# Second attention: q and k projections in three lots of eight, with paired 64-row remainders

## The chip, the cores and the metric

The kernel runs on one core of a Trainium2 chip. The metric is the device time of one execution in microseconds (us). A TensorE (PE) matmul takes a stationary operand of up to 128 x 128, loaded by a weight load (PEld), and a moving operand of up to 128 x 512; results go to PSUM, eight banks of 512 float32 values a partition. VectorE (DVE) and ScalarE (ACT) read PSUM; GpSimd (POOL) and SyncE (SP) work on SBUF and issue transfers (DMAs).

## The reference, cut to what matters

```
x = A_x
x = x + A(layernorm(x), A_wqkv, A_wo)                    # first attention
x = x + B(layernorm(x), B_w_in, B_w_sp, B_b_sp, B_w_out) # feed-forward
x = x + A(layernorm(x), A_wqkv, A_wo)                    # second attention
x = x + B(layernorm(x), B_w_in, B_w_sp, B_b_sp, B_w_out)

def A(x, wqkv, wo):      # x: 2048 x 576, 32 heads of 18, window of 8 positions, dilation 2
    q, k, v = split(x @ wqkv)
    logits = q . k[pos - 2*(0..7)] * scale, masked where the position is negative
    return (softmax(logits) @ v[pos - 2*(0..7)]) @ wo

def B(x, w_in, w_sp, b_sp, w_out):
    z1, z2 = split(gelu(x @ w_in)); g = w_sp @ layernorm(z2) + b_sp
    return (z1 * g) @ w_out
```

## The kernel before

Four layers, A B A B, run one after the other. The normalised input stands transposed in `xnT`: 128 partitions, five chunks of the 576 features, 2048 positions. Four chunks are full; the fifth has 64 features. Its lower 64 partitions hold either a copy of the upper 64 (where the writer of the rows makes one, `dup`) or zeros; `wqk4`, the fifth chunk of the q and k weights, has zeros in its lower 64 rows, so that a full-height matmul of chunk five gives the product of 64 rows.

In an attention layer the engines' order is written by hand. Its pieces:

- `PG(d, qk, cc, ...)`, one unit of the q and k projection: for 128 of the 576 output columns (d = 0 to 4; at d = 4, one unit gives the last 64 of q and of k), q or k, and 512 positions (cc = 0 to 3), five matmuls into one PSUM bank (L436), a copy of the bank into a staging buffer `stg` (`evac`, ACT L404 or DVE L402), and, when all units of a d over 1024 positions are there, about eight DMAs that move each head's 18 rows into `QK` (L78), dealt to the SP and POOL queues. There are four staging buffers, used in turn; a copy into one waits until the moves out of it have landed.
- `fill_window_rows`, DVE copies of a mask pattern into `QK` (L198, L202); the moves into `QK` come after them.
- `VW(t, hh)`, a v product: five matmuls of 288 columns (L410) and a copy into `v_ext`, in this stage on ACT (L404).
- `L_mm(s)`, logits of half a tile: 16 matmuls of 32 rows (L473) into the three-bank buffer `X0` and one "Y" bank; `EXP(s)`, two exponentials on ACT (L482); `PV(s)`, the weighted sum (L496) and the division on DVE.

PSUM in an attention layer: three banks for `X0` (0 to 2), two "Y" (3, 4) and three "PT" (5, 6, 7). `PT_tile` takes a bank for a unit or a v product by the tags in `self.ring`: Y, Y, PT, PT, PT at first, PT alone from the line in front of `L_mm(0)` on. Which buffer of a tag is taken is settled when the program is built.

The second attention (li = 2) starts with 18 units (d = 0 to 4, cc = 0 and 1), then eight v products (tiles 0 to 3), then `L_mm(0)` and `EXP(0)`, then six more units (d = 0 to 2, cc = 2, the list `pre`), then a loop over the steps: at each, `L_mm(s + 1)`, `EXP(s + 1)`, `PV(s)` and what a table puts there (the remaining units, v products, output projection, layer norm).

Ahead of it, the output stage of the first feed-forward (L1104) writes the rows of `xnT` tile by tile: sums, statistics, normalised rows on ACT (`ln_xn`, L253), transposition by DMA. In it the second attention's weights are loaded through ACT's DMA queue (`late_loads`), and `zero_right` (L297) zeroes the lower rows of three weights on DVE.

The feed-forward's first product (`z1`, L1031, and `p1_group`, L907) has the form that the change takes up: chunks one to four of half of the units, then chunk five of all units as half-height matmuls at rows 0 and 64 in turn, which address the two halves of the array, then chunks one to four of the other half.

Of the kernel before, what the change touches and what calls it, by code (L numbers as in the profile page):

```python
# [12 lines left out]
f32 = mybir.dt.float32  # L13
# [5 lines left out]
P = 128  # L19
# [44 lines left out]
class K:  # L64
# [229 lines left out]
        wv = wp.tile([P, 5, D], bf16, name="wv_sb")  # L294
        self.right = dict(pf_cm=pf_cm, w_cm=w_cm, pf=pf, win2a=win2a, wqk=wqk, wqk4=wqk4, wv=wv, wo=wo)

    def zero_right(self):  # L297
        nc, R = self.nc, self.right
        nc.vector.memset(R["wqk4"][64:128, :], 0.0)
        nc.vector.memset(R["wv"][64:128, 4, :], 0.0)  # L300
        nc.vector.memset(R["wo"][64:128, 4, :], 0.0)

    def load_wqk(self, eng):

        R = self.right
        for c0, n, w0 in ((D, 512, D + 64), (0, D, 0), (D + 512, 64, D)):
            self.dma(R["wqk"][:, :, w0:w0 + n], self.A_wqkv[0:512, c0:c0 + n].rearrange("(c p) n -> p c n", p=P), eng=eng)
            self.dma(R["wqk4"][:64, w0:w0 + n], self.A_wqkv[512:576, c0:c0 + n], eng=eng)

    def load_wv(self, eng, nh=1):  # L310
        R, n = self.right, D // nh
# [27 lines left out]
    def layer_A(self, li):  # L339
# [33 lines left out]
        R = self.right  # L373
# [26 lines left out]
        def evac(out, in_, dve):  # L400
            if dve:
                nc.vector.tensor_copy(out=out, in_=in_)  # L402
            else:
                nc.scalar.copy(out=out, in_=in_)  # L404
# [9 lines left out]
        stg_tiles, stg_left = {}, {}  # L414
        dma_rr, stg_rr = [0], [0]

        def PG(d, qk, cc, dve, queues=(nc.sync, nc.gpsimd)):

            cb, gi = divmod(cc, CBW // 512)
            alone = bool(lent) and d == 4 and cb == 1  # L420
            key = (d, cc if alone else cb, alone)
            if key not in stg_tiles:
                if alone:
                    stg_tiles[key] = lent[1]
                elif cb == 0 and d >= 3 and lent:
                    stg_tiles[key] = lent[d - 3]
                else:
                    stg_tiles[key] = stgs[stg_rr[0] % NSTG]
                    stg_rr[0] += 1
                stg_left[key] = 1 if alone else (2 if d < 4 else 1) * (CBW // 512)  # L430
            stg = stg_tiles[key]
            pp = self.PT_tile([P, 512], f32, "pp")
            w0 = d * P + (640 if qk else 0)
            for c in range(5):
                w = wqk[:, c, w0:w0 + P] if c < 4 else wqk4[:, w0:w0 + P]
                nc.tensor.matmul(pp[:, :], lhsT=w, rhs=self.xnT[:, c, cc * 512:(cc + 1) * 512],  # L436
                                 start=(c == 0), stop=(c == 4))
            evac(stg[:, qk, gi * 512:(gi + 1) * 512], pp[:, :], dve)
            stg_left[key] -= 1
            if stg_left[key] == 0:  # L440
                stg_tiles.pop(key)
                cs = slice(cc * 512, (cc + 1) * 512) if alone else slice(cb * CBW, (cb + 1) * CBW)
                ss = slice(gi * 512, (gi + 1) * 512) if alone else slice(0, CBW)
                moves = []
                for h in range(d * P // DH, H):
                    a, b = max(h * DH, d * P), min((h + 1) * DH, (d + 1) * P)
                    if a >= b:
                        break
                    g, rg = divmod(h, 4)
# [153 lines left out]
        if li == 0:  # L603
# [44 lines left out]
            xns = {}  # L648
# [72 lines left out]
            T_(12, 13, 14, 15)  # L721
            nvw0, nvw = 4, 9
        else:
            for k_, (d, cc) in enumerate([(d, cc) for d in range(5) for cc in range(2)]):
                for qk in ((1, 0) if d < 4 else (0,)):
                    PG(d, qk, cc, k_ == 0, (nc.gpsimd, nc.sync) if d == 0 else q2)
                if k_ == 0:
                    self.fill_window_rows(QK, 0)
                    setup_bufs(nc.vector)
                    nc.vector.memset(v_ext[:, :, :, DH:DH + 1], 1.0)  # L730
                    exp_table()
                if k_ == 1:
                    self.run_deferred()
                if k_ == 6:
                    self.fill_window_rows(QK, 1)
            nvw0, nvw = 0, 4
        for t in range(nvw0, nvw - (1 if li == 0 else 0)):
            for hh in range(2):
# [74 lines left out]
            at(s_b + 2 * k_, win2b_piece, k_)  # L813
        at(NST - 2, O_T, NT - 2)
        at(NST, O_T, NT - 1)
        for k_, (d, qk, cc) in enumerate(pre):
            if k_ == (2 if li == 0 else 0):
                self.ring = ["PT"]
                L_mm(0)
                EXP(0)  # L820
            PG(d, qk, cc, li > 0 or k_ < 4, q2)
            if li == 0 and k_ == 3:
                self.fill_window_rows(QK, 1)
# [24 lines left out]
    def layer_B(self, li):  # L848
# [231 lines left out]
        late_loads = []  # L1080
        if next_is_A:
            self.open_right()
            late_loads = [lambda: self.load_wqk(nc.scalar),
                          lambda: self.load_wv(nc.scalar), lambda: self.load_wo(nc.scalar)] + self.load_win2a(nc.scalar)
        xns = {}

# [21 lines left out]
        def p3_finish(i, acc):  # L1108
            xo = p3.tile([P, D], f32, name="xo3", bufs=3)
            self.dma(xo[:], self.rows_of(x_prev, i) if next_is_A else x_prev[i * P:(i + 1) * P, :], eng=nc.sync)  # L1110
            x_new = p3.tile([P, D], bf16 if last else f32, name="x_new3", bufs=3)
            for hh in range(2):
                hs = slice(hh * 288, (hh + 1) * 288)
                nc.vector.tensor_tensor(out=x_new[:, hs], in0=acc[hh], in1=xo[:, hs], op=ALU.add)  # L1114
                if last:
                    self.dma(self.out[i * P:(i + 1) * P, hs], x_new[:, hs], eng=(nc.sync, nc.scalar)[hh])
            if not last:
                self.dma(self.xres[li][i * P:(i + 1) * P, :], x_new[:])
                mv, rstd, nmr = self.ln_stats(p3, x_new, P)
                xns[i] = self.ln_xn(x_new, P, mv, rstd, nmr, eng="act", dup=False)  # L1120
            if i >= 2 and (i - 2) in xns:
                p3_ln_T(i - 2)()

# [11 lines left out]
        for i in range(i0, NS):  # L1135
            pos_ = [self.PT_tile([P, 512], f32, "po") for hh in range(2)]
            acc = [pos_[0][:, 0:288], pos_[1][:, 0:288]]
            p3_mm(i, acc, range(NJ))
            p3_finish(i, acc)
            if next_is_A and i == 2:  # L1140
                self.zero_right()
            if i >= 3 and late_loads:
                late_loads.pop(0)()
        if (NS - 2) in xns:
# [72 lines left out]
```

## Time and profile before

| what | value |
|---|---|
| median of 3 runs | 1165.69 us (1164.6 to 1165.92) |
| profiled execution, first to last instruction | 1170.2 us |
| PE busy | 1150.5 us, 98% of the span, 8163 instructions |
| DVE, ACT, POOL busy | 550.0, 338.8, 278.8 us |
| PE, matmuls of the q and k units (L436), both attentions | x341, 82.2 us, mean 382 ns |
| mean granted PE clock | 0.997 of full |

The profiled execution's own time is known through its span alone; it is 4.5 us above the runs' median. A matmul's recorded length holds its way through the array, so consecutive ones overlap: the pitch from start to start is what counts. A line of the timeline gives start, length, engine, line of the kernel, operation, output and inputs, form, count, and in brackets the idle time before and what ended it. Times are us from the span's start. Some matmul records are missing.

### The profile page before, as it was taken

To read this page: it belongs to the slowest core of one execution; us is meant where nothing else is said; L and a number is where in the kernel's file an instruction comes from. 1 tells how busy PE (TensorE), PEld (TensorE's weight loads), DVE (VectorE), ACT (ScalarE), POOL (GpSimd) and SP (SyncE) were. 2 spreads that over 40 slices of the span, in tenths; PEclk is the share of its full clock that TensorE was granted. 3 is DMA by queue.
4 is the path that set the end of the run, shared out by engine and by line. 5 is a ranking of instruction groups with operands and counts; after the bars stand their busy time and mean duration, and the time that the engine had idled before them with its cause. 6 is when DMAs were issued, how large, how long until landed. Compare 5 with 4: busy or idle time off the path is not lost.

```text
span 1170.2 us, 19968 instructions
## 1 busy us (share of the span) xinstructions
PE 1150.5 (98%) x8163; PEld 612.5 (52%) x8258; DVE 550.0 (47%) x1167; ACT 338.8 (29%) x493; POOL 278.8 (24%) x389
## 2 busy tenths in 40 slices
PE   9999999999999999999999999999999999999998
PEld 5457544444444444457755774444444444444677
DVE  8668598322333332244555886963322223322321
ACT  5589455111100111101247884541011110111000
POOL 4659865000000000001153786640000000000000
PEclk9999999999999999999999999999999999999999
DMA  9599697000000000049646997930000000001332
GB/s 217 119 160 294 193 212 142 23 12 12 12 1 12 12 12 1 6 138 296 169 107 105 204 256 182 242 91 1 12 12 12 12 12 1 12 1 46 111 105 74
DMA packets 183240, 106.45 MB, mean 91 GB/s; under 512 B 135225, under 2 KB 164441, under 8 KB 183149
## 3 DMA queue, kind: packets, MB, share of 16 engines
q1 hardware_dynamic: 170285, 84.85, 31.6%
q0 software_dynamic: 6512, 14.57, 4.8%
q10 hardware_dynamic: 6352, 5.75, 1.6%
q8 instruction: 64, 1.05, 0.4%
q14 instruction: 27, 0.22, 0.1%
HBM read 42.40 MB, written 21.77 MB: 55 GB/s over the span
## 4 chain that ended last, share of the span: by engine, by line
PE 85%; POOL 7%; DMA 3%; DVE 2%; issue 2%; ACT 0%; SPq 0%; POOLq 0%; DVEq 0%; ACTq 0%
PE pg L1055 42%; PE po L1104 12%; PE pz L1031 6%; PE pz1s L1031 6%; PE pzs L907 5%; PE pp L436 4%; PE pz L907 4%; POOL ln_xn L259 4%; PE pv L410 2%; PE O_ps L496 1%; PE pw L557 1%; PE L_ps L473 1%; POOL ln_rstd L582 1%; DMA QK<-stg 1%; DMA o_slot<-o_t 1%
## 5 line engine op out<-in xcount | busy, mean ns | idle before, releaser
L1055 PE MATMUL pg<-Wq,Z 128*128 128x512 bf16 x2260 | 497.9, 379 | 2.5
L1055 PEld LDWEIGHTS <-Z 128*128 128x128 bf16 x2304 | 225.5, 98 | 271.8
L1059 DVE TENSOR_TENSOR g_tmp<-pg,ln_xn 128x512 f32<-128x512 f32 x144 | 99.6, 692 | 421.5 <-PE pg L1055 419.5
L1050 ACT ACTIVATE z1T<-pz 128x1024 bf16<-128x1024 f32 x36 | 34.9, 1021 | 500.8 <-PE pz L1031 500.8
L78 POOL DMA_DIRECT2D wout<-in_B_w_out_dram x4 | 4.3, 1070 | 598.8 <-PE pg L1055 598.8
L1104 PE MATMUL po<-wout,Z 128*128 128x288 bf16 x1152 | 141.4, 286 | 0.0
L482 ACT ACTIVATE P_sb<-L_ps 128x1440 bf16<-128x1440 f32 (+3 forms) x136 | 125.1, 972 | 21.1 <-PE L_ps L473 19.7
L1104 PEld LDWEIGHTS <-Z 128*128 128x128 bf16 x1152 | 112.7, 98 | 28.8
L907 PEld LDWEIGHTS <-xnT 128*128 128x128 bf16 (+1 forms) x800 | 68.7, 98 | 80.0 <-issue 15.5
L1060 DVE TENSOR_TENSOR Z<-g_tmp,z1T 128x512 bf16<-128x512 f32 x144 | 99.7, 692 | 12.2
L956 DVE BATCH_NORM_STATS2 z_st<-zp 128x6 f32<-128x512 bf16 (+1 forms) x160 | 91.0, 617 | 5.1 <-ACT zp L954 4.8
L1031 PEld LDWEIGHTS <-w 128*128 128x128 bf16 (+1 forms) x640 | 53.7, 97 | 74.0 <-issue 13.6
L436 PE MATMUL pp<-xnT,wqk_sb 128*128 128x512 bf16 x341 | 82.2, 382 | 2.5 <-DVE o_t L504 1.3
L259 POOL TENSOR_SCALAR ln_xn<-x_new,ln_mv,ln_rstd 128x576 bf16<-128x576 f32 x32 | 73.3, 2291 | 2.6
L1114 DVE TENSOR_TENSOR x_new<-po,xo 128x288 f32<-128x288 f32 (+1 forms) x64 | 28.8, 455 | 87.4 <-PE po L1104 83.9
L1031 PE MATMUL pz<-xnT,w 128*128 128x512 bf16 (+1 forms) x316 | 66.3, 380 | 0.2
L1031 PE MATMUL pz1s<-xnT,w 128*128 128x512 bf16 (+1 forms) x310 | 64.9, 379 | 0.9 <-issue 0.8
L78 POOL DMA_DIRECT2D QK<-stg x81 | 49.5, 614 | 46.0 <-DVE oT L524 14.8
L907 PE MATMUL pzs<-win2a,xnT 128*128 128x512 bf16 (+1 forms) x235 | 59.9, 364 | 0.4 <-issue 0.3
L907 PE MATMUL pz<-win2a,xnT 128*128 128x512 bf16 (+1 forms) x233 | 58.3, 357 | 0.6 <-issue 0.2
L980 POOL TENSOR_SCALAR Z<-zp,z_mv,z_rstd 128x256 bf16<-128x256 bf16 x32 | 55.7, 1740 | 3.4
L436 PEld LDWEIGHTS <-wqk_sb 128*128 128x128 bf16 x360 | 33.5, 98 | 38.3 <-DVE o_t L504 1.5
(113 smaller groups left out, 936.6 us busy)
## 6 DMA issues: line engine op xcount, KB each, us to landing
xres<-x_new SPq DMA_DIRECT2D x48, 288.0 KB
xo<-xres SPq DMA_DIRECT2D x32, 288.0 KB
wout<-in_B_w_out_dram POOLq DMA_DIRECT2D x4, 1296.0 KB, 8.2
xn_rows<-ln_xn SPq DMA_DIRECT2D x32, 160.0 KB
w<-in_B_w_in_dram SPq DMA_DIRECT2D x16, 256.0 KB
QK<-stg POOLq DMA_DIRECT2D x55, 72.0 KB, 5.2
xo<-xres SPq DMA_DIRECT2D x6, 576.0 KB
QK<-stg SPq DMA_DIRECT2D x39, 72.0 KB
```

The lines of the kernel that those rows point to most:

```text
L78: return eng.dma_start(out=out, in_=in_)
L259: e.tensor_scalar(out=xn[:nrows, 0:D], in0=x_t[:nrows, :], scalar1=mv[:nrows, 0:1], scalar2=rstd[:nrows, 0:1], op0=ALU.subtract, op1=ALU.mult)
L436: nc.tensor.matmul(pp[:, :], lhsT=w, rhs=self.xnT[:, c, cc * 512:(cc + 1) * 512], start=(c == 0), stop=(c == 4))
L482: nc.scalar.activation(out=P_bufs[2 * jp + s % 2][:nk, :, :, 0:nq], in_=Lv[:nk, :, :, 0:nq], func=ACT.Exp, scale=scale)
L907: nc.tensor.matmul(out[:, o0:o0 + n], lhsT=self.xnT[r0:r1, c, r * P:(r + 1) * P], rhs=win2(c)[r0:r1, w0:w0 + n], start=start, stop=stop, t ...
L956: nc.vector.bn_stats(out=st[:, x // 512, :], in_=zp[:, x:x + min(512, w0 + n - x)])
L980: eng.tensor_scalar(out=Z[:, b0:b1, i, :], in0=zv[:, b0:b1, :], scalar1=mv[:, 0:1], scalar2=rstd[:, 0:1], op0=ALU.subtract, op1=ALU.mult)
L1031: nc.tensor.matmul(outs[a_], lhsT=w1[r0:r1, c, sub * P:(sub + 1) * P], rhs=self.xnT[r0:r1, c, q * 512:(q + 1) * 512], start=start, stop=st ...
L1055: nc.tensor.matmul(pg[:, :], lhsT=Z[:, jj, i, sub * P:(sub + 1) * P], rhs=Wq[q][:, i, :], start=(i == 0), stop=(i == NS - 1))
L1059: nc.vector.tensor_tensor(out=tmp[:], in0=pg[:, :], in1=bsp[:, qs], op=ALU.add)
L1060: nc.vector.tensor_tensor(out=uT(jj)[:, sub, qs], in0=tmp[:], in1=z1Ts[jj, sub][:, qs], op=ALU.mult)
L1104: nc.tensor.matmul(acc[hh], lhsT=u_rows(j, i), rhs=wouts[j // NJH][:, j % NJH, hh * 288:(hh + 1) * 288], start=(j == 0), stop=(j == NJ - 1))
```

## The change

In the second attention alone, the first 24 units (the 18 and the six of `pre`) are put into three lots of eight, `PG_run`. A lot takes all eight banks (`PG_banks`: the three of `X0`, and five of the ring). In it, the first four units run chunks one to four; then all eight run chunk five as half-height matmuls, units 0, 2, 4, 6 on rows 0 to 63 and units 1, 3, 5, 7 on rows 64 to 127; the first four are copied out; the last four run chunks one to four and are copied out. Lots one and two are copied by ACT, lot three by DVE.

For this the lower 64 rows of `xnT`'s fifth chunk and of `wqk4` must hold copies: `ln_xn` in the output stage before makes its copy of 64 columns (one more ACT instruction for each of 16 tiles), the three pieces of `wqk4` are loaded twice, and the DVE memset of `wqk4` goes. Behind the third lot a POOL memset zeroes `wqk4`'s lower rows, since the loop's units go on with full-height matmuls.

Around it: the window rows of the first half are filled ahead of the first unit instead of behind the second; buffer set-up, the exponential's table and the deferred transposition stand behind lot one, the window rows of the second half behind lot two. `self.ring = ["PT"]`, `L_mm(0)` and `EXP(0)` now follow lot three, and the eight v products follow them.

```diff
-    def zero_right(self):
+    def zero_right(self, wqk=True):
         nc, R = self.nc, self.right
-        nc.vector.memset(R["wqk4"][64:128, :], 0.0)
+        if wqk:
+            nc.vector.memset(R["wqk4"][64:128, :], 0.0)
...
-            self.dma(R["wqk4"][:64, w0:w0 + n], self.A_wqkv[512:576, c0:c0 + n], eng=eng)
+            for r in ((0, 64) if twice else (0,)):
+                self.dma(R["wqk4"][r:r + 64, w0:w0 + n], self.A_wqkv[512:576, c0:c0 + n], eng=eng)
...
+        def PG_mm(pp, d, qk, cc, c, start, stop, half=None):
+            w0 = d * P + (640 if qk else 0)
+            r0, r1 = (0, P) if half is None else (64 * half, 64 * half + 64)
+            w = wqk[:, c, w0:w0 + P] if c < 4 else wqk4[r0:r1, w0:w0 + P]
+            nc.tensor.matmul(pp, lhsT=w, rhs=self.xnT[r0:r1, c, cc * 512:(cc + 1) * 512],
+                             start=start, stop=stop, tile_position=(r0, 0))
+
+        def PG_run(units, banks, between=None):
+            n = len(units) // 2
+            for u in range(n):
+                for c in range(4):
+                    PG_mm(banks[u], *units[u][:3], c, c == 0, False)
+            for u in range(2 * n):
+                PG_mm(banks[u], *units[u][:3], 4, u >= n, u < n, half=u % 2)
+            for u in range(n):
+                PG(*units[u], pp=banks[u])
+            for u in range(n, 2 * n):
+                for c in range(4):
+                    PG_mm(banks[u], *units[u][:3], c, False, c == 3)
+                PG(*units[u], pp=banks[u])
+
+        def PG_banks():
+            return ([X0[:, k_, :] for k_ in range(3)] +
+                    [self.PT_tile([P, 512], f32, "pp")[:, :] for k_ in range(5)])
...
-            pp = self.PT_tile([P, 512], f32, "pp")
-            w0 = d * P + (640 if qk else 0)
-            for c in range(5):
-                w = wqk[:, c, w0:w0 + P] if c < 4 else wqk4[:, w0:w0 + P]
-                nc.tensor.matmul(pp[:, :], lhsT=w, rhs=self.xnT[:, c, cc * 512:(cc + 1) * 512],
-                                 start=(c == 0), stop=(c == 4))
-            evac(stg[:, qk, gi * 512:(gi + 1) * 512], pp[:, :], dve)
+            if pp is None:
+                pp = self.PT_tile([P, 512], f32, "pp")[:, :]
+                for c in range(5):
+                    PG_mm(pp, d, qk, cc, c, c == 0, c == 4)
+            evac(stg[:, qk, gi * 512:(gi + 1) * 512], pp, dve)
...
-            for k_, (d, cc) in enumerate([(d, cc) for d in range(5) for cc in range(2)]):
-                for qk in ((1, 0) if d < 4 else (0,)):
-                    PG(d, qk, cc, k_ == 0, (nc.gpsimd, nc.sync) if d == 0 else q2)
+            prol = [(d, qk, cc) for d in range(4) for cc in range(2) for qk in (1, 0)] + [(4, 0, 0), (4, 0, 1)]
+            prol += [(d, qk, 2) for d in range(3) for qk in (1, 0)]
+            self.fill_window_rows(QK, 0)
+            for k_ in range(0, 24, 8):
+                PG_run([(*u, k_ == 16, (nc.gpsimd, nc.sync) if u[0] == 0 and u[2] < 2 else q2)
+                        for j, u in enumerate(prol[k_:k_ + 8])], PG_banks())
                 if k_ == 0:
-                    self.fill_window_rows(QK, 0)
                     setup_bufs(nc.vector)
                     nc.vector.memset(v_ext[:, :, :, DH:DH + 1], 1.0)
                     exp_table()
-                if k_ == 1:
                     self.run_deferred()
-                if k_ == 6:
+                if k_ == 8:
                     self.fill_window_rows(QK, 1)
+            nc.gpsimd.memset(wqk4[64:128, :], 0.0)
+            self.ring = ["PT"]
+            L_mm(0)
+            EXP(0)
             nvw0, nvw = 0, 4
...
-        for k_, (d, qk, cc) in enumerate(pre):
-            if k_ == (2 if li == 0 else 0):
+        for k_, (d, qk, cc) in enumerate(pre if li == 0 else ()):
+            if k_ == 2:
                 self.ring = ["PT"]
                 L_mm(0)
                 EXP(0)
...
-            late_loads = [lambda: self.load_wqk(nc.scalar),
+            late_loads = [lambda: self.load_wqk(nc.scalar, twice=True),
...
-                xns[i] = self.ln_xn(x_new, P, mv, rstd, nmr, eng="act", dup=False)
+                xns[i] = self.ln_xn(x_new, P, mv, rstd, nmr, eng="act")
...
-                self.zero_right()
+                self.zero_right(False)
```

More of the change, by code (lines that the diff above doesn't have):

```diff
@@ L295, in open_right, with load_wqk @@
         self.right = dict(pf_cm=pf_cm, w_cm=w_cm, pf=pf, win2a=win2a, wqk=wqk, wqk4=wqk4, wv=wv, wo=wo)
-    def zero_right(self):
+    def zero_right(self, wqk=True):
         nc, R = self.nc, self.right
-        nc.vector.memset(R["wqk4"][64:128, :], 0.0)
+        if wqk:
+            nc.vector.memset(R["wqk4"][64:128, :], 0.0)
         nc.vector.memset(R["wv"][64:128, 4, :], 0.0)
         nc.vector.memset(R["wo"][64:128, 4, :], 0.0)
-    def load_wqk(self, eng):
+    def load_wqk(self, eng, twice=False):
         R = self.right
@@ L415, in layer_A, with PG @@
         dma_rr, stg_rr = [0], [0]
-        def PG(d, qk, cc, dve, queues=(nc.sync, nc.gpsimd)):
+        def PG_mm(pp, d, qk, cc, c, start, stop, half=None):
[20 more added lines that the diff above has]
+                    [self.PT_tile([P, 512], f32, "pp")[:, :] for k_ in range(5)])
+        def PG(d, qk, cc, dve, queues=(nc.sync, nc.gpsimd), pp=None):
             cb, gi = divmod(cc, CBW // 512)
```

## The prediction

> **What bounds the kernel now.** I read the chain of waits first: 85% of the span hangs on TensorE (PE).
>
> ```profile
> PE 85%; POOL 7%; DMA 3%; DVE 2%; issue 2%; ACT 0%; SPq 0%; POOLq 0%; DVEq 0%; ACTq 0%
> ```
>
> So what the change does is settled at its own place, the start of the second attention. There I read the timeline (start, length, engine, line, operation, count, idle time before).
>
> ```profile
> 592.98 19.59 PE L436 MATMUL pp<-xnT,wqk_sb 128*128 128x512 bf16 x88
> ...
> 612.40 5.06 PE L410 MATMUL pv<-wv_sb,xnT 128*128 128x288 bf16 x40
> 613.21 0.40 ACT L404 CAST v_ext<-pv 128x288 bf16<-128x288 f32 x1
> 613.83 0.40 ACT L404 CAST v_ext<-pv 128x288 bf16<-128x288 f32 x1 [0.21 <-PE pv L410]
> ...
> 617.40 0.40 PE L473 MATMUL L_ps<-QK 32*128 32x128 bf16 x16
> ...
> 617.73 6.65 PE L436 MATMUL pp<-xnT,wqk_sb 128*128 128x512 bf16 x29
> 617.84 1.94 ACT L482 ACTIVATE P_sb<-L_ps 128x1536 bf16<-128x1536 f32 x2
> ...
> 624.31 0.40 PE L473 MATMUL L_ps<-QK 32*128 32x128 bf16 x16
> ```
>
> The reader is to see five blocks back to back on PE: 18 q and k units (90 matmuls, a few of them missing from the records) from 592.98 to 612.40; eight v products, 40 matmuls, to 617.30; the first logits at 617.40; six more units from 617.73; the second logits at 624.31. One 512-column matmul costs (612.40 - 592.98)/90 = 0.216 us, a v product (617.30 - 612.40)/8 = 0.61 us. PE does not wait for ScalarE (ACT) here: the v copies follow the products at the same 0.61 us and hold nothing up. The stretch I forecast is 592.98 to 624.31, 31.33 us.
>
> A delay at 624.31 stays. From there the logits are tied to the exponentials, because one three-bank buffer holds them:
>
> ```profile
> 624.81 11.48 ACT L482 ACTIVATE P_sb<-L_ps 128x1536 bf16<-128x1536 f32 x12 [5.03 <-PE L_ps L473]
> 626.31 0.39 PE L473 MATMUL L_ps<-QK 32*128 32x120 bf16 x16
> 628.23 0.39 PE L473 MATMUL L_ps<-QK 32*128 32x120 bf16 x16
> ...
> 660.00:670.00 10.00, 10.00 (x205) 7.33 (x202) 8.71 (x31) 9.60 (x13) 7.59 (x10) 1.00 0.99 224
> ```
>
> Twelve activations, six steps, take 11.48 us without a hole, 1.91 us a step, the pitch of the logits; later PE itself is full (10.00 of 10 us from 660 to 670, the second column of that row). Neither has room to catch up, so whatever moves 624.31 moves the end.
>
> **The lots.** 24 units of five matmuls become 24 of four, plus 24 half-height matmuls in 12 pairs. The kernel already does this in the feed-forward's z1 stage, four full units, eight halves, four full units, the same 40 instructions as one lot:
>
> ```profile
> L1031 PEld LDWEIGHTS <-w x40: 93/98/99, 882.4 to 890.2; 128*128 128x128 bf16 x32, 64*128 64x128 bf16 x8
> ...
> 882.63:886.08 3.45, 3.40 (x15) 1.47 (x15) 1.00 0.01 2
> 886.18:887.05 0.87, 0.87 (x9) 0.30 (x8) 1.00 0.00 0
> 887.15:890.62 3.47, 3.47 (x18) 1.48 (x16) 1.00 0.00 0
> ```
>
> Eight halves take 0.87 us, as long as four full matmuls: the pairs do run side by side. A tenth is lost at each change of height (886.08 to 886.18, 887.05 to 887.15). A lot takes 890.62 - 882.63 = 7.99 us against 40 x 0.216 = 8.63; three lots 23.96 against 25.90. **Gain: 1.94 us**, 0.17% of the run and no more. As for bounds: with pairs that did not overlap it would be a loss of the switches, 3 x 0.2; nothing in the rows allows a gain over 12 x 0.216 = 2.6.
>
> Can the lots wait? Lot 2 needs the banks of lot 1. ACT copies eight units in a lot of 7.99 us at 0.59 each, 4.7 us, and the first four are copied while PE runs the last sixteen matmuls. Lot 3 is copied by VectorE (DVE), 8 x 0.69 = 5.5 us, into staging buffers whose moves into QK must have landed.
>
> ```profile
> 601.45 13.66 POOL L78 DMA_DIRECT2D QK<-stg  x19 [5.75 <-ACT stg L404]
> ...
> 612.65 0.59 ACT L404 CAST stg<-pp 128x512 bf16<-128x512 f32 x1 [0.55 <-PE pp L436]
> ...
> 619.08 0.69 DVE L402 CAST stg<-pp 128x512 bf16<-128x512 f32 x1 [11.06 <-DMA QK<-stg]
> ```
>
> Their issues fill the GpSimd (POOL) queue, 0.72 us each; in the new order they start one to two us earlier, since the window rows are filled ahead of the first unit. The last two copies may still wait for the moves of d = 3, as the 619.08 row shows such a wait; they guard the banks of the seventh and eighth v product only, which come late (below). Cost 0, bounds 0 to 1.5 us.
>
> **The v products, which stand outside the diff.** Before, they stood between the units, over five banks. Now they stand behind the first logits, and the ring of banks is cut to the three "PT" banks before them. In the changed program as built, the eight go to banks 5, 5, 5, 5, 5, 5, 7, 6 (before: 7, 6, 3, 4, 5, 7, 6, 3), and the second to sixth each wait for ACT:
>
> ```
> Matmult pv<-wv_sb,xnT 128x288 [waits DVE]         first
> Matmult pv<-wv_sb,xnT 128x288 [waits Activation]  second to sixth
> Matmult pv<-wv_sb,xnT 128x288 [waits DVE]         seventh, eighth
> ```
>
> So product and copy, which overlapped, alternate; and ahead of the first copy on ACT now stand the two exponentials of the first logits. Worked out on the clock of this trace: lots end at 592.98 + 23.96 = 616.94, logits at 617.04 (the 0.10 from 617.30 to 617.40), exponentials 0.44 later (617.84 - 617.40) for 1.94 us, to 619.42. The first v product (617.37) is done by then; its copy ends at 619.82. The second product starts 0.05 after it (624.81 + 1.45 = 626.26 to 626.31, where the logits waited for an exponential in the same manner; the 1.45 is the row below). From there one turn is 0.82 us from the first matmul to the copy (612.40 + 0.61 = 613.01 to 613.83), 0.40 copy and 0.05 back: 1.27 against 0.61. That a v product waits for a v copy is nothing new to this kernel: the first attention has one such wait, the 39.00 row.
>
> ```profile
> 617.84 1.45 ACT L482 ACTIVATE P_sb<-L_ps 128x1536 bf16<-128x1536 f32 x1
> ...
> 39.00 2.48 PE L410 MATMUL pv<-wv_sb,xnT 128*128 128x288 bf16 x14 [2.47 <-DVE v_ext L402]
> ```
>
> Products two to six start at 619.87, 621.14, 622.41, 623.68, 624.95; the last two follow at 0.61 and end at 626.78; the second logits start at 626.88 instead of 624.31: **+2.57 us, the gain of 1.94 already taken off** (the stall alone is 4.5). The exponential behind them is queued after the last copy, which ends (626.17 + 0.82 + 0.40 = 627.39) just as the logits are ready, so it adds nothing.
>
> **The clock.** PE then is idle from about 618.1 to 619.9, and for 0.5 of each turn of 1.27 until 625.6. The windows with the granted clock (column after the engines) show what that may bring:
>
> ```profile
> 36.71:40.12 3.41, 1.12 (x10) 0.89 (x10) 2.54 (x7) 0.31 (x1) 3.41 (x7) 1.00 0.67 167
> 40.12:43.53 3.41, 3.19 (x12) 1.62 (x11) 0.46 (x1) 0.49 (x2) 3.41 (x6) 0.50 0.77 176
> ...
> 145.94:149.35 3.41, 2.20 (x15) 0.81 (x13) 3.38 (x7) 1.84 (x4) 2.15 (x3) 1.00 0.70 139
> 149.35:152.77 3.42, 3.42 (x9) 1.21 (x9) 3.39 (x8) 1.73 (x3) 2.31 (x4) 0.50 0.52 115
> 722.80:726.21 3.41, 2.66 (x14) 1.00 (x12) 3.38 (x7) 2.28 (x4) 2.05 (x4) 1.00 0.65 136
> ...
> 147.94 1.37 PE L907 MATMUL pzs<-win2b,xnT 64*128 64x512 bf16 x5 [0.97 <-ACT zp L954]
> ```
>
> Where PE was busy 1.12 or 2.20 of 3.41 us, the next 3.41 us ran at half clock; with 2.66 busy they did not. In the new stretch a window of 3.41 us holds, by the times above, between 1.2 us (from 618 on) and some 2.3 us of work, whichever way the windows fall. So I take one window at half clock. In it a turn costs 0.61 more (its five matmuls take twice the 0.61), 1.88 us; 3.41/1.88 = 1.8 turns, **+1.1 us**. Bounds: 0, and two such windows, the second of them in the loop, up to 3.41/2 = 1.7 more.
>
> The Trainium skill, "TensorE: Matmul & The Clock Gate" (the table of what to do about the clock gate), asks only for no idle gap over about 3 us between bursts. By that rule the clock would hold here and the term would be 0; the trace speaks against it, as the 0.97 us hole at 147.94 was enough, in a window busy 64%.
>
> **Small edits.** They hang beside other work:
>
> ```profile
> L253 ACT ACTIVATE ln_xn<-x_new,ln_nmr,ln_rstd 128x576 bf16<-128x576 f32 x16 | 13.9, 867 | 87.1 <-POOL ln_nmr L243 44.7 <-DVE x_new L1114 38.9 <-DMA xres<-x_new 3.5
> ...
> L160 POOL MEMSET win_pat<- 128x528 bf16 x1 | 0.5, 538 | 0.0
> ...
> 524.14 2.94 ACTq L78 DMA_DIRECT2D wqk_sb<-in_A_wqkv_dram  x5
> ```
>
> Sixteen copies of 64 columns on ACT (under the 0.40 of a 288-column one) fit into its 87.1 us of idle there. Three more weight DMAs add 3 x 0.59 = 1.8 us to ACT's queue 60 us ahead of their use; without that cover the first layer-norm row would be late by 1.8. The POOL memset of 64 x 1152 costs 0.54 to 1.2 us by the 528-column row; it queues behind the last moves of d = 4, about 618, and the loop's first unit needs it at 628. The VectorE memset that goes away was not on the path. All 0; if one of them stood on the path, up to 1.
>
> **Sum.** -1.94 + 4.51 + 1.1 = +3.7 us. On the profiled span, 1170.2, that is 1173.9; the runs' median, 1165.69, lies 4.5 us below that span, and I lay the same difference on it: 1169.4.
>
> **The rivals.** *The clock holds* (20%): everything else as above, +2.57, 1168.3. For it: only two windows in this trace were cut, and products at 0.61 in 1.27 are close to the 2.66 that was spared. Against: the first window has the hole of 1.8 us in it. *The gain stands alone* (6%): the copies turn out not to hold PE, as in the before trace, and the lots bring 1165.69 - 1.94 = 1163.7, not slower. It decides if the v products do not share a bank; for it speaks only that no row of this stage shows such a wait, against it the order as built and the 39.00 row. *More than one window, or the copies of lot 3 late* (16%): a second window at half clock, or a staging wait that delays the first v product beyond 618.6; +5.4, 1171.1. Pairs that do not overlap are excluded by the 886.18 row.
>
> **How the numbers follow.** Forecast 58%, the rivals as given. A difference under 0.2%, 2.3 us, can't be told from no change. Slower by more: nearly all of the forecast and of the late case, 0.6 of the held clock, 85%. Within: 0.4 of the held clock and most of the lone gain, 12%. Faster: 3%, since the gain alone, 1.94, is short of the bound. The range takes in the held clock with its scatter and half of the late case: 1167.4 to 1171.6.
>
> **What would show it.** Right: pp blocks of 7.99 us a lot; the first logits 0.4 us earlier against the first unit; 1.27 us from product to product in the first six v products, "ACT v_ext" named as what PE waited for; one window of clock 0.5 behind them; the second logits 2.6 to 3.7 us later. Wrong: v products at 0.61 us, logits early by 1.9, or idle PE inside a lot, waiting for a copy or for landed moves.

## The result, and the profile after

| | median of the runs | ratio to before, 95% interval |
|---|---|---|
| before, 10 runs beside the changed kernel | 1167.32 us (1164.6 to 1170.15) | |
| changed kernel, 10 runs | 1176.17 us (1168.46 to 1184.5) | 1.008 [1.0052, 1.0109] |

The change makes the kernel 8.9 us slower, 0.8%. The forecast was 1169.4 us, 3.7 us slower, range 1167.4 to 1171.6: the direction is right, the size is not, and the time lies outside the range. The three runs of before that the forecast was laid on had a median 1.6 us under that of the ten; the rest of the miss is in the change.

The runs of the changed kernel scatter over 16 us, and with them their mean granted clock. The two at 0.999 and 1.000 took 1168.46 and 1171.71 us; the other eight, at 0.991 to 0.996, 1173.99 to 1184.5. The clock is not all of the scatter: those two differ by 3.3 us, and before's ten runs lie 5.6 us apart. The profiled run is one in the middle (span 1176.6 us, clock 0.994).

The timeline of PE over the stretch of the forecast, from the first matmul of the units to the second logits (start, length, engine, line, operation, form, count, idle time before it; units of a lot that stand in the banks of `X0` go by the name `L_ps`):

```profile
590.78 2.75 PE L423 MATMUL L_ps<-xnT,wqk_sb 128*128 128x512 bf16 x12
...
599.71 2.75 PE L423 MATMUL L_ps<-xnT,wqk_sb 128*128 128x512 bf16 x12 [0.78 <-ACT stg L406]
...
607.69 2.75 PE L423 MATMUL L_ps<-xnT,wqk_sb 128*128 128x512 bf16 x12
...
615.77 0.40 PE L498 MATMUL L_ps<-QK 32*128 32x128 bf16 x16
618.54 0.77 PE L412 MATMUL pv<-wv_sb,xnT 128*128 128x288 bf16 x5 [2.38 <-DVE stg L404]
619.80 1.00 PE L412 MATMUL pv<-wv_sb,xnT 128*128 128x288 bf16 x5 [0.49 <-ACT v_ext L406]
621.29 1.36 PE L412 MATMUL pv<-wv_sb,xnT 128*128 128x288 bf16 x5 [0.49 <-ACT v_ext L406]
...
626.83 3.76 PE L412 MATMUL pv<-wv_sb,xnT 128*128 128x288 bf16 x15 [0.49 <-ACT v_ext L406]
630.52 0.40 PE L498 MATMUL L_ps<-QK 32*128 32x128 bf16 x16
```

Before, the stretch was 31.33 us (592.98 to 624.31); now it is 630.52 - 590.78 = 39.74, 8.41 more. The profiled spans differ by less, 1176.6 - 1170.2 = 6.4 us, since outside the stretch it is the profile of before that is 2.0 us longer; it has two windows at half clock there (at 40.12 and 149.35), the changed kernel's one (at 39.95). So the loss lies in the stretch. It can be laid beside the forecast of 31.33 + 3.67 = 35.0 part by part:

| part | forecast | measured | difference |
|---|---|---|---|
| lot 1, to the first matmul of lot 2 | 7.99 | 599.71 - 590.78 = 8.93 | +0.94 |
| lots 2 and 3, to the first logits | 16.07 | 615.77 - 599.71 = 16.06 | 0 |
| logits to the second v product | 2.83 | 619.80 - 615.77 = 4.03 | +1.20 |
| second v product to the second logits | 7.01 + 1.1 | 630.52 - 619.80 = 10.72 | +2.61 |

Where the first two differences come from stands on the other engines, in the timelines of DVE, POOL and ACT:

```profile
592.35 4.62 DVE L198 COPY QK<-win_pat 128x4096 bf16<-128x4096 bf16 x4
...
592.58 2.16 POOL L239 TENSOR_TENSOR ln_rstd<-ln_rstd,neg_half 128x1 f32<-128x1 f32 x1 [3.50 <-DVE ln_rstd L238]
594.84 2.18 POOL L243 TENSOR_SCALAR ln_nmr<-ln_mv,ln_rstd 128x1 f32<-128x1 f32 x1
...
597.05 0.87 ACT L253 ACTIVATE ln_xn<-x_new,ln_nmr,ln_rstd 128x576 bf16<-128x576 f32 x1 [6.80 <-DVE QK L202]
...
598.10 1.55 ACT L406 CAST stg<-L_ps 128x512 bf16<-128x512 f32 x3
...
600.43 11.04 POOL L78 DMA_DIRECT2D QK<-stg  x15 [3.41 <-ACT stg L406]
...
617.20 1.29 DVE L404 CAST stg<-pp 128x512 bf16<-128x512 f32 x2 [2.78 <-DMA QK<-stg]
```

The window rows, now filled ahead of the first unit, are copied by DVE just while POOL does two steps on a single column for the last row tile of the layer norm. Each takes 2.2 us. So that tile's `ln_xn` starts at 597.05. Before, it started 0.95 us after POOL's first step (595.73 - 594.78), which would be 593.53 here: 3.5 us late. The copies of lot 1 stand behind it in ACT's order and start at 598.10, lot 2 waits for its first bank, and the moves out of staging start 600.43 - 590.78 = 9.65 us behind the first matmul (before: 601.45 - 592.98 = 8.47). The bracket of 597.05 names DVE because its last fill ended at about the same time as POOL's step; what the activation reads is `ln_nmr`.

Late moves make DVE's copies of lot 3 late. The two at 617.20, of the fifth and sixth unit, waited for moves to land, and the first v product takes the bank of the sixth unit. That is the hole of 2.38 us at 618.54.

The last difference is the clock. Windows of 3.41 us: PE, PEld, DVE, ACT and POOL busy, then the granted clock, DMA share, GB/s:

```profile
616.80:620.22 3.42, 1.19 (x9) 0.82 (x9) 1.29 (x2) 1.80 (x3) 2.49 (x5) 1.00 0.42 90
620.22:623.63 3.41, 2.43 (x11) 1.20 (x10) 1.29 (x2) 0.80 (x2) 0.43 (x1) 0.50 0.01 2
623.63:627.05 3.42, 2.44 (x11) 1.21 (x10) 0.00 (x0) 0.80 (x2) 0.00 (x0) 0.50 0.00 0
627.05:630.46 3.41, 3.41 (x15) 1.89 (x13) 0.00 (x0) 0.80 (x2) 0.00 (x0) 0.50 0.00 0
```

Three windows at half clock, 10.24 us, cover nearly all of the time from the second v product to the last. A turn, one product and its copy one after the other on bank 5, takes 1.85 us in them (623.14 to 624.99, say) instead of the first one's 1.26 (618.54 to 619.80).

### The profile page after: what moved, and what is told of

The parts are those of the page before. It is cut to its first block, busy times and chain, and to the rows that moved or that the text cites. A ratio compares the mean times of both kernels' runs of the same rounds, so it can differ in the third digit from the quotient of the medians.

```text
span 1176.6 us, 20068 instructions
## 1 busy us (share of the span) xinstructions
PE 1156.6 (98%) x8258; PEld 611.7 (52%) x8258; DVE 549.2 (47%) x1166; ACT 341.8 (29%) x509; POOL 282.0 (24%) x390
## 3 DMA queue, kind: packets, MB, share of 16 engines
q8 instruction: 64, 1.05, 0.4%
## 4 chain that ended last, share of the span: by engine, by line
PE 84%; POOL 7%; DMA 4%; DVE 3%; issue 1%; ACT 1%; SPq 0%; DVEq 0%; POOLq 0%; ACTq 0%
PE pg L1085 42%; PE po L1134 12%; PE pz L1061 6%; PE pz1s L1061 6%; PE pzs L937 5%; PE pz L937 5%; POOL ln_xn L259 3%; PE pv L412 2%; DMA QK<-stg 2%; POOL QK L78 2%; PE pp L423 1%; PE O_ps L521 1%; PE pw L582 1%; DVE QK L198 1%; PE L_ps L498 1%
## 5 line engine op out<-in xcount | busy, mean ns | idle before, releaser
L423 PE MATMUL pp<-xnT,wqk_sb 128*128 128x512 bf16 (+1 forms) x315 | 73.1, 381 | 1.3 <-DVE o_t L529 1.3
L412 PE MATMUL pv<-wv_sb,xnT 128*128 128x288 bf16 x340 | 55.0, 304 | 7.6 <-DVE v_ext L404 2.6
```

The costliest lines, as they stand in the source:

```text
L412: nc.tensor.matmul(pv[:nk, 0:288], lhsT=self.xnT[:, c, k0_(t):k0_(t) + nk], rhs=wv_sb[:, c, hh * 288:(hh + 1) * 288], start=(c == 0), stop ...
L423: nc.tensor.matmul(pp, lhsT=w, rhs=self.xnT[r0:r1, c, cc * 512:(cc + 1) * 512], start=start, stop=stop, tile_position=(r0, 0))
```

## The experiments

The stretch, first matmul of the units to second logits, is read in each profile in the same way; the loop behind it goes on at 1.91 us a step. A stretch is that of one profile, a median that of four (e4_busy), five (e6_turns) or eight to twelve runs; the profiled runs of e1_banks and e2_nmr were the fastest of their kernels, 3.2 and 2.7 us under the median. Against the kernel before:

| | edit | stretch | against 31.33 | median against before's beside it | ratio |
|---|---|---|---|---|---|
| after | | 39.74 | +8.41 | +8.85 | 1.008 [1.0052, 1.0109] |
| e1_banks | v products on four banks | 35.00 | +3.67 | +4.09 | 1.0047 [1.0028, 1.0065] |
| e2_nmr | last `ln_nmr` on DVE, ahead of the fill | 33.81 | +2.48 | +2.76 | 1.0033 [1.0018, 1.0048] |
| e3_both | both | 30.70 | -0.63 | -1.91 | 0.9989 [0.9975, 1.0003] |
| e4_busy | after, gaps of PE filled | 38.09 | +6.76 | +5.88 | 1.0061 [1.0046, 1.0076] |
| e5_full | e3_both without pairs | 31.34 | +0.01 | -1.04 | 1.0 [0.9981, 1.0019] |
| e6_turns | after, only the turns filled | 37.07 | +5.74 | +5.20 | 1.0042 [1.0023, 1.0061] |
| e7_queue | e3_both, some moves issued by ACT | 33.67 | +2.34 | +3.97 | 1.003 [1.0016, 1.0045] |
| e8_order | e3_both, two v copies on DVE | 29.74 | -1.59 | -2.08 | 0.9978 [0.9963, 0.9992] |
| e9_fill | before, only the fill moved ahead | 32.99 | +1.66 | +1.28 | 1.0012 [0.9992, 1.0031] |

### The v products on four banks

```diff
+                bk = PG_banks()
...
-                        for j, u in enumerate(prol[k_:k_ + 8])], PG_banks())
+                        for j, u in enumerate(prol[k_:k_ + 8])], bk)
...
-                VW(t, hh, li == 0 and hh == 0)
+                VW(t, hh, li == 0 and hh == 0, bk[4 + (2 * t + hh) % 4] if li > 0 else None)
```

> The eight v products go round the last four banks of lot 3 (4, 5, 7, 6) instead of bank 5. Theory (the stretch lost its time to four things: last row of the layer norm late 0.9, copies of lot 3 late behind the moves out of staging 1.2, turns of product and copy, half clock in those turns): lot 2 still idles 0.8 us, the first and the third v product still wait for VectorE's copies of lot 3 (some 2 and 4.5 us behind the logits), but none waits for a v copy; from the third on 0.61 us each; first pp matmul to second logits 34 us instead of 39.74, clock 0.5 in one window at most, median about 1170. Rival (the half clock comes from the hole behind the logits and not from the turns): v products at 1.2 us each, two or three windows of 0.5, stretch 36 to 38, median 1173.

The timeline of PE in e1_banks:

```profile
613.10 1.39 PE L413 MATMUL pp<-wv_sb,xnT 128*128 128x288 bf16 x10 [1.88 <-DVE stg L404]
615.78 5.11 PE L413 MATMUL pp<-wv_sb,xnT 128*128 128x288 bf16 x30 [1.30 <-DVE stg L404]
620.82 0.40 PE L499 MATMUL L_ps<-QK 32*128 32x128 bf16 x16
```

The window at half clock in it:

```profile
615.03:618.44 3.41, 2.66 (x12) 1.64 (x12) 1.29 (x2) 0.47 (x2) 0.58 (x1) 0.50 0.04 11
```

No v product waits for a v copy any more; the first and the third wait for DVE, as the theory has it. Six products at 0.61 would take 3.7 us and took 5.1: one window at half clock, in which PE still had 2.66 us of work. The stretch is 1 us longer than expected, the median 1170.99 instead of some 1170. Sharing bank 5 costs 39.74 - 35.00 = 4.74 us here, with the part of the clock that hangs on it; the holes alone cost one window.

### The last row of the layer norm

```diff
-        nc.gpsimd.tensor_scalar(out=nmr[:nrows, :], in0=mv[:nrows, 0:1], scalar1=rstd[:nrows, 0:1], scalar2=-1.0,
+        (nmr_eng or nc.gpsimd).tensor_scalar(out=nmr[:nrows, :], in0=mv[:nrows, 0:1], scalar1=rstd[:nrows, 0:1], scalar2=-1.0,
...
-                mv, rstd, nmr = self.ln_stats(p3, x_new, P)
+                mv, rstd, nmr = self.ln_stats(p3, x_new, P, nmr_eng=nc.vector if i == NS - 1 else None)
```

On DVE the `ln_nmr` step (586.85 to 587.06) waits for POOL's first step, and the fill stands behind it: it now starts at 586.98, when POOL's first step (586.27, 0.55 us) is done.

> Only the last row's ln_nmr moves from GpSimd to VectorE, ahead of the window rows' fill in VectorE's order, so that the fill can't run beside GpSimd's two small steps. Theory: ln_rstd takes 0.55 us again instead of 2.16, the last ln_xn starts 3.5 us earlier, lot 2 follows lot 1 without the 0.78 us of idle (8.0 a lot), the moves out of staging start 2 us earlier and the first v product starts within 0.5 us of the logits; the turns of 1.27 to 1.85 stay. Stretch 39.74 - 0.9 - 1.2 = 37.6, less if a half-clock window goes with it (36); median 1173 to 1174.5. Rival (the copies of lot 3 are late for the number of moves, not for their start): lot 2 without idle, but first v product still 2.4 us behind the logits, stretch 38.8, median 1175.

Timelines of POOL and of PE in e2_nmr:

```profile
586.27 0.55 POOL L239 TENSOR_TENSOR ln_rstd<-ln_rstd,neg_half 128x1 f32<-128x1 f32 x1 [3.50 <-DVE ln_rstd L238]
592.49 1.93 POOL L78 DMA_DIRECT2D QK<-stg  x3 [5.67 <-ACT stg L406]
```

```profile
584.46 2.75 PE L423 MATMUL L_ps<-xnT,wqk_sb 128*128 128x512 bf16 x11
...
592.45 2.54 PE L423 MATMUL L_ps<-xnT,wqk_sb 128*128 128x512 bf16 x11
...
608.51 0.40 PE L498 MATMUL L_ps<-QK 32*128 32x128 bf16 x16
609.86 0.77 PE L412 MATMUL pv<-wv_sb,xnT 128*128 128x288 bf16 x5 [0.95 <-DVE stg L404]
611.29 0.77 PE L412 MATMUL pv<-wv_sb,xnT 128*128 128x288 bf16 x5 [0.66 <-ACT v_ext L406]
...
618.27 0.40 PE L498 MATMUL L_ps<-QK 32*128 32x128 bf16 x16
```

One instruction of 0.2 us put elsewhere takes 5.9 us off the stretch. The step on POOL is back at 0.55, lot 2 follows lot 1 after 7.99, the moves start 8.0 us behind the first matmul, the hole behind the logits is 0.95 instead of 2.38. In this profile the clock stays full in the stretch, with the turns still there, at 1.26 us. Seven of its ten runs have a mean clock of 0.999 or 1.000; the other three, at 0.994 to 0.997, may have had a cut here. The expectation, 36 to 37.6 and a median of 1173 to 1174.5, was too careful: in the profile all of the cut went, not one window of it, and the median is 1169.66.

This profile is the forecast's own rival "the clock holds": it has what was reckoned for the lots, the exponentials and the turns, 31.33 + 2.57 = 33.90 against 33.81 measured, and a median 2.76 us above before.

### Both

> Both edits. Theory: lots 8.0 us each, v products at 0.61 us with short waits for VectorE's copies, no window of 0.5 in the stretch; first pp matmul to second logits 30 to 31.3 us against 31.33 before the change, so the time is at the one before or 1 us under it: 1165.5 to 1167.5. Rival (something outside the stretch was lost too): stretch as said, but 1170 or more.

Timelines of DVE and PE in e3_both:

```profile
613.87 1.29 DVE L404 CAST stg<-pp 128x512 bf16<-128x512 f32 x2 [1.32 <-ACT P_sb L508]
614.62 3.83 PE L413 MATMUL pp<-wv_sb,xnT 128*128 128x288 bf16 x30 [1.16 <-DVE stg L404]
618.38 0.40 PE L499 MATMUL L_ps<-QK 32*128 32x128 bf16 x16
```

PE has one wait over 0.2 us left, 1.16 us at the third v product, for DVE's copy of the seventh unit of lot 3 (the first of the two at 613.87). The trace names an exponential as what that copy waited for, which it does not read; that it is the staging buffer, still held by the moves of d = 3, is worked out from the order of the buffers. The stretch, 587.68 to 618.38, is 30.70 us, as expected; the median is 1164.99 against 1166.9, 0.5 under the expected range, with an interval that just reaches no change. So nothing of weight was lost outside the stretch.

### The clock by itself

e4_busy and e6_turns are meant to leave every wait of the changed kernel and put unread matmuls into PE's gaps.

```diff
                 VW(t, hh, li == 0 and hh == 0)
+                for _ in range(2 if li > 0 and 2 * t + hh < 5 else 0):
+                    nc.tensor.matmul(bk[4], lhsT=wqk[:, 0, 0:P], rhs=self.xnT[:, 0, 0:512], start=True, stop=True)
```

This is e6_turns; e4_busy has also eight of them behind the logits, and another spare bank.

> As after, with matmuls that nobody reads in the gaps of TensorE: eight of 512 columns behind the first logits, two behind each of the first five v products, into a spare bank. They change no wait. Theory (holes in TensorE's work cut its clock): no window of 0.5 behind the logits, turns of 1.27 to 1.4 us, first v product to second logits 8.3 us instead of 11.98; stretch 39.74 - 3.7 = 36.0, median 1172.5. Rival (the clock is cut for another reason, or the extra work draws it down): windows of 0.5 remain and the turns stay at 1.85 or grow; median 1176 or more.

> As after (fill ahead, hole of 2.4 us behind the logits, bank 5 for the first v products), with two unread 512-column matmuls behind each of the first five v products only, into a bank that is free by then; so the turns are full and the hole stays. Theory A (hole and turns together cut the clock): mean clock 0.998 or more in most runs, turns 1.26, the times of the runs within 4 us of each other, stretch 36 to 37, median 1171 to 1172. Theory B (the hole alone cuts it): one or more windows of 0.5 behind the hole in most runs, mean clock 0.994 to 0.997, turns of 1.85 and more, median 1176.

Windows that hold the hole or the turns, on the grid on which each run's clock changes, in e4_busy, then in e6_turns, then in e2_nmr for comparison:

```profile
608.23:611.65 3.42, 1.55 (x22) 0.69 (x21) 0.78 (x2) 1.78 (x2) 2.37 (x5) 1.00 0.74 132
```

```profile
611.48:614.89 3.41, 1.43 (x22) 0.62 (x20) 0.89 (x2) 1.88 (x2) 2.31 (x5) 1.00 0.73 131
614.89:618.30 3.41, 2.96 (x11) 1.58 (x11) 1.69 (x3) 0.46 (x2) 2.06 (x3) 0.50 0.18 45
618.30:621.71 3.41, 3.18 (x18) 1.74 (x18) 0.00 (x0) 1.21 (x3) 0.00 (x0) 1.00 0.00 0
```

```profile
610.13:613.55 3.42, 2.05 (x15) 1.23 (x13) 1.29 (x2) 1.70 (x5) 1.92 (x3) 1.00 0.14 36
613.55:616.96 3.41, 2.17 (x16) 1.46 (x16) 0.00 (x0) 1.01 (x3) 0.00 (x0) 1.00 0.00 0
```

With the turns full (e6_turns) the hole still cuts the clock, but for one window instead of three, and the turns after it are back at 1.26; with the turns open and a hole of 0.95 (e2_nmr) nothing is cut. So in the changed kernel the hole starts the cut and the turns, which leave PE idle for 0.98 of 3.41 us even at half speed, keep it up: in every profile here a half-clock window with 2.66 or more of work was the last, and the two with 2.43 and 2.44 were not. The five runs of e6_turns lie between 1168.35 and 1173.37 with clocks of 0.998 to 1.000, so most of the 16 us of scatter went with the longer cut. Theory A had the turns, once the window is over, and the median right, the stretch (37.07 for 36 to 37) and the scatter (5 us for 4) nearly; that the hole alone still costs one window is theory B's share.

e4_busy has no window of 0.5 in the stretch and turns of 1.26, but a stretch of 38.09, not 36.0: its spare bank was held by the first exponential, so the eight matmuls started 2.08 us late and pushed the first v product to 4.21 us behind the logits (2.77 in the changed kernel). Without these 1.44 us it is 36.65.

### The fill by itself

In the kernel before, `self.fill_window_rows(QK, 0)` goes from behind the second unit to ahead of the first; nothing else.

> The kernel before, with only the first filling of the window rows moved ahead of the first unit, as the change has it; no lots. Theory (the fill slows GpSimd's two small steps of the last layer-norm row): ln_rstd and ln_nmr take about 2.2 us each, the last ln_xn starts 3.3 us later, the first two units' copies on VectorE start 4.6 us later; five banks are full after 5.4 us, so TensorE idles 1.5 us in the first ten units; stretch 31.33 + 1.5 = 32.8, median 0.1% above the kernel before. Rival (in after it was the lots that made GpSimd late): ln_rstd and ln_nmr at 0.55 and 0.27 us, ln_xn on time, stretch 31.3 to 32.1.

Timelines of POOL and PE in e9_fill, and of DVE and POOL in the kernel before at the same place:

```profile
590.80 2.16 POOL L239 TENSOR_TENSOR ln_rstd<-ln_rstd,neg_half 128x1 f32<-128x1 f32 x1 [3.50 <-DVE ln_rstd L238]
593.05 2.18 POOL L243 TENSOR_SCALAR ln_nmr<-ln_mv,ln_rstd 128x1 f32<-128x1 f32 x1
...
596.05 14.19 PE L436 MATMUL pp<-xnT,wqk_sb 128*128 128x512 bf16 x64 [1.50 <-DVE stg L402]
```

```profile
594.55 1.48 DVE L402 CAST stg<-pp 128x512 bf16<-128x512 f32 x2
...
594.78 0.55 POOL L239 TENSOR_TENSOR ln_rstd<-ln_rstd,neg_half 128x1 f32<-128x1 f32 x1 [3.50 <-DVE ln_rstd L238]
595.43 0.27 POOL L243 TENSOR_SCALAR ln_nmr<-ln_mv,ln_rstd 128x1 f32<-128x1 f32 x1
```

The two steps take the same 2.16 and 2.18 us without any lot, and PE idles the 1.50 us that were expected, five banks against a first copy at 595.32. Beside DVE's copies out of PSUM the steps took 0.55 and 0.27. So it is the fill, a copy from SBUF to SBUF, and it is not the lots. By the stretch this edit alone costs 1.66 us; its ratio, 1.0012, is not clear of no change.

### What the pairs are worth

```diff
-                PG_mm(banks[u], *units[u][:3], 4, u >= n, u < n, half=u % 2)
+                PG_mm(banks[u], *units[u][:3], 4, u >= n, u < n)
```

> e3_both with the fifth matmul of each unit of the lots at full height instead of pairs of halves (it so adds the 64-row remainder twice; loads, order and banks stay). It measures the pairs by themselves. Theory: a lot takes 40 x 0.216 = 8.63 us instead of 7.98, so the first logits come 1.9 us later after the first matmul; of that the waits for VectorE's copies of lot 3 give back 1.2, since these copies are then on time: stretch 30.70 + 0.8 = 31.5 to 32.6, median 1166 to 1167. Rival (pairs hardly overlap): lots of 8.0 to 8.2, stretch 31.

Timelines of PE and DVE in e5_full:

```profile
586.02 2.75 PE L424 MATMUL L_ps<-xnT,wqk_sb 128*128 128x512 bf16 x11
...
594.65 2.54 PE L424 MATMUL L_ps<-xnT,wqk_sb 128*128 128x512 bf16 x11
...
612.02 0.40 PE L499 MATMUL L_ps<-QK 32*128 32x128 bf16 x16
612.25 1.29 DVE L404 CAST stg<-pp 128x512 bf16<-128x512 f32 x2 [0.93 <-PE pp L424]
612.35 5.07 PE L413 MATMUL pp<-wv_sb,xnT 128*128 128x288 bf16 x40
617.36 0.40 PE L499 MATMUL L_ps<-QK 32*128 32x128 bf16 x16
```

A lot of full matmuls takes 8.63 us, 0.65 more than with pairs: the gain of 1.94 for three lots is there. But these slower lots leave PE no wait at all: eight v products in 5.0 us, stretch 31.34, which is before's 31.33 and a little under the 31.5 to 32.6 expected. Against them e3_both is only 0.64 us better; the other 1.3 go into the wait for the seventh unit's copy. That copy comes 26.2 us behind the first matmul in both (612.25 - 586.02 and 613.87 - 587.68): in e3_both the faster lots reach it earlier and wait.

### Two ways to get at the rest

In e7_queue ACT issues the moves of d = 3 (`(nc.scalar,) if u[0] == 3`).

> e3_both with the moves of d = 3 out of staging issued by ScalarE, which is idle from the last copy of lot 2 to the first exponential, instead of GpSimd and SyncE. Theory (what is left of the wait in e3_both, 1.16 us, is the queueing of the moves): GpSimd's run of 22 moves ends 3 us earlier, VectorE's copies 5 to 8 of lot 3 follow the matmuls, no TensorE idle over 0.3 us between the logits, stretch 29.5 to 29.9, median 1164, below the kernel before by 0.2 to 0.3%. Rival (the moves' landing is bound by the transfers and not by their issue): copies as late as in e3_both, stretch 30.7, median 1165.

The timeline of ACT's queue, DVE and PE in e7_queue:

```profile
603.59 7.64 ACTq L78 DMA_DIRECT2D QK<-stg  x8
...
614.30 1.29 DVE L404 CAST stg<-pp 128x512 bf16<-128x512 f32 x2 [3.60 <-ACT v_ext L406]
...
615.04 5.51 PE L413 MATMUL pp<-wv_sb,xnT 128*128 128x288 bf16 x30 [2.46 <-DVE stg L404]
```

A miss. ACT starts behind its last copy of lot 2 and takes 0.96 us an issue (POOL 0.74 in the changed kernel, 11.04/15). DVE's last two copies come 27.5 us behind the first matmul instead of 26.2. The hole grew to 2.46 us and a half-clock window followed it; the profile has a second one outside the stretch, at 694.08, and a mean clock of 0.997, as nine of the eleven runs have. Whether issue or landing sets the end of these moves stays open.

In e8_order the last two copies of lot 3 are held back till DVE has copied the first two v products, and the v products use the banks of the fifth and sixth unit, which are free earlier, for the first four:

```diff
-                VW(t, hh, li == 0 and hh == 0, bk[4 + (2 * t + hh) % 4] if li > 0 else None)
+                v_ = 2 * t + hh
+                VW(t, hh, (li == 0 and hh == 0) or (li > 0 and v_ < 2), bk[(4, 5, 4, 5, 6, 7, 4, 5)[v_]] if li > 0 else None)
+                if li > 0 and v_ == 1:
+                    for f in held:
+                        f()
```

> e3_both with VectorE copying the first two v products ahead of the last two units of lot 3, and the v products on the banks 4, 5, 4, 5, 6, 7, 4, 5 of these units, so that the third no longer waits for the unit whose staging buffer is late. Theory (the pairs' gain is there, but lands in the wait for staging): no TensorE idle over 0.3 us between the first and the second logits, stretch 29.4 to 29.8 against 31.33 before the change, median 0.15 to 0.25% below the kernel before. Rival (another wait comes in its place, the copies by VectorE or ScalarE): third or fifth v product late by 0.5 us or more, stretch 30.2 or more, median as e3_both.

The timeline of PE in e8_order:

```profile
587.47 2.75 PE L424 MATMUL L_ps<-xnT,wqk_sb 128*128 128x512 bf16 x11
...
611.52 0.40 PE L501 MATMUL L_ps<-QK 32*128 32x128 bf16 x16
612.03 5.25 PE L413 MATMUL pp<-wv_sb,xnT 128*128 128x288 bf16 x40
617.21 0.40 PE L501 MATMUL L_ps<-QK 32*128 32x128 bf16 x16
```

Forty matmuls of v in one row of the timeline, no wait over 0.2 us, stretch 29.74: 1.59 us less than before and 1.60 less than e5_full. The median is 2.08 us under before's, 0.9978 [0.9963, 0.9992]: with three things around them put right (the clash with the fill, the banks, the order of the copies) the lots are faster than the kernel before, by 0.2%. That it is the pairs that pay rests on the stretches, one profile each; by the medians e5_full and e8_order can't be told apart for sure, since their intervals overlap.

## Why the prediction was wrong

- **The lots** (right). 7.98 us for lots 2 and 3 against 7.99 forecast; pairs side by side; 1.94 us as worked out, measured as three times 0.65 in e5_full.
- **"Can the lots wait?", cost 0** (wrong; the first step that failed). The sum of ACT's copying time was right, but not its start. The forecast took the fill ahead of the first unit as a help ("they start one to two us earlier") and never set it beside what POOL was then doing. Moves started 1.2 us later instead, and lot 1 lasted 0.94 longer; PE waiting for a copy (0.78 us at 599.71) was among the signs of being wrong that the prediction named. e9_fill shows the slowing without the rest of the change, e2_nmr shows that keeping the fill and the steps apart takes 5.9 us off the stretch.
- **"They guard the banks of the seventh and eighth v product only", 0 to 1.5 us** (wrong). The built order of banks was in the prediction, 5 for the first six, but not held against which unit of lot 3 frees bank 5. It is the sixth, whose staging buffer is late: the first v product waited, 1.20 us beyond the exponentials. With the moves on time (e2_nmr) 0.95 us of hole remains, which the exponentials would have cost at the second product anyway.
- **The v products' turn, 1.27 us, and the net +2.57** (right). 1.26 in e2_nmr, net +2.48. e1_banks confirms the cause: on four banks no product waits for a v copy.
- **The clock, one window, +1.1** (mis-sized). Three windows; from the second v product to the second logits 10.72 us against 6.98 at full clock in e2_nmr, so 3.74. The forecast counted windows by PE's share of busy time and gave the second to the loop at most; it did not ask whether PE at half speed, with the same waits, would be busy enough to get out again.
- **The small edits, 0** (right for the ones named). The copies of 64 columns and the POOL memset (619.60, 1.05 us, ahead of its use at 631.27) show no waiter, and with those copies in place lot 1 takes 7.99 in e2_nmr. The fill was not counted among them.

The forecast gave 20% to the held clock and 16% to a second window or late copies. The latter came, both halves of it at once, and at 8.4 instead of 5.4 us, since the two are not apart: a late copy makes the hole that starts the cut. That the change would be slower was no luck: with the clash with the fill out of the way, in e2_nmr, it still is, by 2.76 us, for the reason that the forecast gave. The largest share, 5.9 of 8.4 us, hangs on a single moved line, by a chain over every engine: POOL late, ACT late, moves late, DVE late, PE idle, clock cut. The shares overlap, though: e2_nmr takes off 5.93 us and e1_banks 4.74, both together 9.04, since each by itself already shortens the cut or ends it.

## What to carry to other kernels

When work is moved ahead on an engine that seemed idle, look at what every other engine does in that very interval, the small single-column steps too, and follow the queue behind them. When a stage is made faster, ask what drains it; a gain that ends in a wait may cost more than it brought, if windows at half clock follow the hole, as they did here. And after a change to a pool's ring, hold the bank each tile gets against the copy that frees it.

## What the runs showed of the hardware

**A copy on VectorE held GpSimd.** POOL's steps of 0.55 and 0.27 us became 2.16 and 2.18 us beside four copies from SBUF to SBUF of 4.62/4 = 1.16 us each. They ended at 594.74 and 597.02, the second and the fourth copy at 594.70 and 596.97, in the changed kernel; so POOL's steps seem not to have run slowly but to have stood till a copy ended. The Trainium skill, "SBUF — State Buffer" (Who interferes with whom), says that VectorE in a mode with two ports and GpSimd contend for a pair of ports that they share: whoever issues first has it for the whole instruction, and the other fully blocks. The ends of the steps agree with a block, which lasted over two copies for each step and not only over the one in progress; in which mode the copies ran, no trace here shows.

**The clock.** The hole before the cut was 2.38 us, and 1.88, 2.43 and 2.46 us in e1_banks, e6_turns and e7_queue, each followed by a window at half clock; the 2.08 us in e4_busy, with dense work behind them, were not. In this stretch a window at full clock with 1.43 us of PE work or less was followed by one, a window with 1.55 or more was not. Elsewhere this does not hold: in e4_busy a window with 1.76 us of work and a hole of 2.07 was followed by one, at 696.98; and at the same place of the first feed-forward a window with 2.20 was followed by one before the change (149.35), one with 2.24 after it (145.77 to 149.18) was not. Neither busy time nor the length of the hole alone settles it, and these runs leave open what does. The Trainium skill, "TensorE: Matmul & The Clock Gate" (A second HAM failure mode: psum-queue depth-cycling), describes a kernel whose clock swings because TensorE idles briefly between groups while it cycles through PSUM banks. The turns on bank 5 leave such brief gaps (0.49 us each), and here they prolonged a cut that a longer hole had begun; by themselves, in e2_nmr's profile, they started none.
